# Weighted phase of a mixture-of-experts kernel: the first product by 20 block products for 24, in ten double steps an item

## The chip, the cores and the metric

The kernel runs on one core of a Trainium2 chip. A core has TensorE (PE, matrix products into PSUM), VectorE (DVE), ScalarE (ACT), GpSimd (POOL) and SyncE (SP, which issues most of the DMA transfers). The metric is the device time of one launch in microseconds, the median of three runs.

## The reference

Linear attention with a polynomial sketch makes the tokens x (4352 x 128); then a routing matrix P is normalised over 8 rounds, and 8 experts are applied densely to every token and weighted by P. The second half matters here:

```python
logits = x @ w_gate
P = np.exp(logits - logits.max())
for _ in range(8):
    P /= P.sum(1, keepdims=True) + 1e-09
    P /= P.sum(0, keepdims=True) + 1e-09
    P *= N / E
for e in range(E):                       # 8 experts, D = 128, F = 1024
    h = np.maximum(x @ w1[e], 0.0)       # first product
    ye = h @ w2[e]                       # second product
    out += P[:, e:e + 1] * ye
```

All is float32. As P is positive, P[:, e] can be multiplied into x before the first product.

## The kernel before

Three stages follow each other. Until about 183 us of the profile, attention and routing are computed, with the experts that need no weight before the first product mixed in as filling (`fill`, `steps`). The rest is the **weighted phase** (`weighted`, line 1088 on), which the change rewrites.

**Items.** The weighted phase handles a list `witems` of 60 pairs (group of tokens g, expert e). A group has 2n tokens: groups 0 to 4 have n = 256 and 7 experts each (items 0 to 34), groups 5 to 8 have n = 224 and 6 experts (items 35 to 58), and a last one has n = 224 and a single expert (item 59). Neighbouring groups run through the experts in opposite directions, so an expert's weights serve two items at a border.

**The first product of an item** is x (2n tokens, 128 inputs) by w1 (128 inputs, 1024 columns). Inputs are cut into two halves of 64 rows, tokens into two blocks of n, and columns into blocks; a fast scheme of the 2 x 2 x 2 kind computes 7 products of sums for 8. `firsts(t)` does one half of the columns (s = 0 or 1) of an item, so each item has two such turns of 7 *steps*. A step is four matmuls of 64 x 64 weights, in the four quarters of the PE array, with n moving columns each (in float32 each is issued as two instructions, so a step shows as x8). The steps alternate between two PSUM pairs (`pairs`); after each step ACT or DVE takes the pair out: ACT copies (lines 1204, 1208, 1211) and ReLUs (1135), and DVE's TENSOR_ADD_SAT (line 1138, shown as CUSTOM_DVE_ANT_0), which adds a PSUM operand and a copy and applies the ReLU. A pair can be written again only when it was taken out.

**The second product** (`seconds`, matmuls of line 1271) is also 7 steps for each half; `seconds(t - 1)` alternates step by step with `firsts(t)`. It needs four differences of h, made by DVE (lines 1181 to 1186), whose operands both lie in SBUF.

**Operands of the first product.** `weigh(i + 2, ...)` multiplies the tokens by the row of P on POOL (line 1048), and two DMAs swap the halves of the partitions (line 1051); `sum_x` makes four sums of x, one double sum on POOL (line 1056) and two on DVE (lines 1058, 1060). x has three buffers (`xf`). Before such a POOL operation stands a `gate`: ACT copies one element of the step's output over an element that the POOL operation writes (line 1148), so POOL's operation can't start before that step.

Sums of w1 (*forms*) are made once for each expert, in the seven items of group 0 (`fresh`): `load_raw` (line 936, four DMAs) brings the raw blocks, `sum_first` (lines 960 to 964) makes the sums on POOL, and `store_first` stores seven forms to DRAM. Later items load them back (`load_first`, line 940), in pieces as soon as a step has read the room. There are two buffers of forms (`w1x`), used in turn.

**Order.** In the weighted phase the order of every engine's queue is the order of the code. Each queue is in order: a waiting instruction holds up those behind it. SP's DMAs stand in the same program order. Just before the phase, operands of items 0 and 1 are made ready (the lines from `open_forms()` on), where a planner orders SP and POOL. When a group ends, `finish_seven` and `out_of` make some ten sums of finished results as `leisure`; POOL (in `aside`, once an item half and twice in the last groups) and DVE (in `spare`) take them one by one; `chores` multiply earlier results by their weights on POOL.

Of the kernel before, what the change touches and what calls it, by code (L numbers as in the profile page):

```python
# [52 lines left out]
def kernel(  # L53
# [849 lines left out]
    late = []  # L903
    forms, form_stores, weights, sources = {}, {}, {}, {}
    FORM = FO * H2 // 2

    PLACE = {f: n for n, f in enumerate((0, 4, 5, 7, 6, 2, 3, 1))}
# [3 lines left out]
    def open_forms():  # L911
        w1 = [late[0].tile([P, 8, FORM], F32, name=f"w1x{k}", bufs=1) for k in range(2)]
# [17 lines left out]
    def load_raw(i):  # L930
        w, e = forms[i], witems[i][1]
        for r in range(2):
            for k in range(2):
                rows = H2 * (r ^ k)
                a, b = PLACE[2 * k], PLACE[2 * k + 1]
                nc.sync.dma_start(out=w[0][H2 * r:H2 * (r + 1), a:b + 1:b - a],
                                  in_=moe_w1[e][rows:rows + H2].rearrange("p (i r n) -> p r i n", i=2, r=2)[:, r])
# [18 lines left out]
    def sum_first(i, parts=(0, 1)):  # L956
        g = nc.gpsimd
        w1 = {f: forms[i][0][:, n] for f, n in PLACE.items()}
        if 0 in parts:
            g.tensor_tensor(w1[4], w1[1], w1[3], op=Alu.add)  # L960
            g.tensor_tensor(w1[6], w1[0], w1[1], op=Alu.subtract)
        if 1 in parts:
            g.tensor_tensor(w1[5], w1[4], w1[0], op=Alu.subtract)
            g.tensor_tensor(w1[7], w1[2], w1[5], op=Alu.subtract)

    def store_first(i):
        nc.sync.dma_start(out=form_stores[witems[i][1]][0], in_=forms[i][0][:, 0:7])

    def second_forms():
# [9 lines left out]
        for e in range(1, E):  # L979
            form_stores[e] = (dram.tile([P, 7, FORM], F32, name=f"w1x{e}"),  # L980
# [61 lines left out]
    def weigh(i, gate):  # L1042

        lo, n, _ = wgroups[witems[i][0]]
        xf = sources[i] = late[0].tile([P, 8 * NW], F32, tag="xf", name="xf", bufs=3)[:, 0:8 * n].rearrange(
            "p (b n) -> p b n", b=8)
        gate(xf[:, 0, 0:1])
        nc.gpsimd.tensor_tensor(xf[:, 0:2].rearrange("p b n -> p (b n)"), xT[:, lo:lo + 2 * n], weights.pop(i),  # L1048
                                op=Alu.mult)
        for s in range(2):  # L1050
            in_turn(i, nc.sync.dma_start(out=xf[H2 * (1 - s):H2 * (2 - s), 2:4], in_=xf[H2 * s:H2 * (s + 1), 0:2]))

    def sum_x(i, part_):
        xf = sources[i]
        if part_ == 0:
            nc.gpsimd.tensor_tensor(xf[:, 4:6], xf[:, 1:4:2], xf[:, 0:2], op=Alu.subtract)  # L1056
        elif part_ == 1:
            nc.vector.tensor_tensor(xf[:, 6], xf[:, 3], xf[:, 4], op=Alu.subtract)
        else:
            nc.vector.tensor_tensor(xf[:, 7], xf[:, 2], xf[:, 6], op=Alu.subtract)  # L1060
# [27 lines left out]
    def weighted():  # L1088
# [4 lines left out]
        copies = late[0].tile([P, 2, 3, 2 * NW], F32, name="copies", bufs=1)  # L1093
        leisure, chores = [(lambda engine, do=do: do(), False) for do in left], []
        acc, counts, ending = {}, {}, []
        todo = [(i, s) for i in range(len(witems)) for s in range(2)]

        def flat(t, n):
            return t.rearrange("p (r n) -> p r n", r=2)

        def rooms(t):
            n = wgroups[witems[todo[t][0]][0]][1]
            base = hb[:, 4096 * (t % 2):4096 * (t % 2 + 1)]
            return [base[:, 2048 * a:2048 * a + 8 * n].rearrange("p (b n) -> p b n", b=4) for a in range(2)]

        def firsts(t):

            i, s = todo[t]
            g, e = witems[i]
            n = wgroups[g][1]  # L1110
            a, c = pairs[::-1] if t % 2 and i else pairs
            w1, xf = forms[i][0], sources[i]
            h, ts = rooms(t)
            pa, pc = a[:, :, 0:n], c[:, :, 0:n]
            p1, p5, u2 = (copies[:, t % 2, m, 0:2 * n] for m in range(3))

            def product(out, form, x, start, stop):
                for r in range(2):
                    rows = slice(H2 * r, H2 * (r + 1))
                    for col in range(2):  # L1120
                        o = P * s + H2 * col
                        nc.tensor.matmul(out[H2 * col:H2 * (col + 1), r], w1[rows, PLACE[form], o:o + H2], xf[rows, x],  # L1122
                                         start=start, stop=stop, tile_position=(H2 * r, H2 * col), skip_group_check=True)

            coming = next_of(i, 2) if s else None

            def fetch(lo, hi):
                if coming is not None and coming not in fresh:
                    load_first(coming, lo, hi)

            def add(out, x, y):
                nc.vector.tensor_tensor(flat(out, n), x, flat(y, n), op=Alu.add)

            def relu(x, y):
# [476 lines left out]
```

## Time and profile before

| | before |
|---|---|
| median of 3 runs | 885.81 us (885.80 to 885.93) |
| profiled execution | 886.26 us, of which the profile's span is 884.4 |
| granted TensorE clock, mean | 1.00 |
| DMA, mean over the span | 202 GB/s |
| weighted phase, first to last step of PE | about 188.9 to 879 us |

How to read it: the page comes from one execution. PE, PEld (weight loads, which overlap PE), DVE, ACT and POOL are engines; "x" is a count of instructions; an arrow `out<-in` names the tiles. In a list by time a row has its start, its length (or that of a merged run), engine, line, operation and tiles, and in brackets the idle time before it and what ended it. Successive DVE or POOL operations can overlap by some hundredths of a microsecond, so start-to-start is the better cost of one in a run. The chain that ended last is followed back from the last instruction to whatever released each step.

### The profile page before, as it was taken

To read this page: it belongs to the slowest core of one execution; us is meant where nothing else is said; L and a number is where in the kernel's file an instruction comes from. 1 tells how busy PE (TensorE), PEld (TensorE's weight loads), DVE (VectorE), ACT (ScalarE), POOL (GpSimd) and SP (SyncE) were. 2 spreads that over 40 slices of the span, in tenths; PEclk is the share of its full clock that TensorE was granted. 3 is DMA by queue.
4 is the path that set the end of the run, shared out by engine and by line. 5 is a ranking of instruction groups with operands and counts; after the bars stand their busy time and mean duration, and the time that the engine had idled before them with its cause. 6 is when DMAs were issued, how large, how long until landed. Compare 5 with 4: busy or idle time off the path is not lost.

```text
span 884.4 us, 36157 instructions
## 1 busy us (share of the span) xinstructions
PE 879.0 (99%) x15308; PEld 655.6 (74%) x15308; DVE 762.0 (86%) x1344; ACT 402.9 (46%) x854; POOL 270.0 (31%) x317
## 2 busy tenths in 40 slices
PE   9999999999999999999999999999999999999998
PEld 6788656878887777677767777767877887877786
DVE  8699689977888988888888888888899899899986
ACT  3455457644444344444344344344444444444443
POOL 3131116444451232322222322331332232242411
PEclk9999999999999999999999999999999999999999
DMA  8889299887886776476667777665775975875871
GB/s 256 273 282 272 76 226 249 131 243 209 239 265 201 238 206 200 138 216 204 182 154 204 205 183 198 194 181 161 231 227 150 256 223 146 233 237 138 238 206 31
DMA packets 146465, 179.08 MB, mean 202 GB/s; under 512 B 55680, under 2 KB 93440, under 8 KB 145920
## 3 DMA queue, kind: packets, MB, share of 16 engines
q1 hardware_dynamic: 138192, 166.30, 65.6%
q0 software_dynamic: 6720, 10.19, 5.7%
q8 instruction: 121, 1.98, 1.0%
q10 hardware_dynamic: 1392, 0.28, 0.2%
q14 instruction: 40, 0.33, 0.1%
HBM read 134.22 MB, written 25.99 MB: 181 GB/s over the span
## 4 chain that ended last, share of the span: by engine, by line
PE 98%; DMA 1%; SPq 0%; DVE 0%; issue 0%
PE pair L1122 39%; PE s L1271 39%; PE a L772 9%; PE s L836 7%; PE a L336 1%; PE a L465 1%; DMA qx<-in_q_dram 0%; DMA v<-in_v_dram 0%; PE a L429 0%; PE a L306 0%; PE s L395 0%; PE s L1287 0%; PE s L375 0%; PE a L499 0%; SPq L173 0%; PE a L375 0%
## 5 line engine op out<-in xcount | busy, mean ns | idle before, releaser
L1122 PE MATMUL pair<-xf,w1x 64*64 64x256 f32 (+1 forms) x6736 | 498.6, 366 | 0.0
L1122 PEld LDWEIGHTS pair<-xf,w1x 64*64 64x64 f32 x6736 | 258.5, 133 | 88.9 <-DVE hb L1138 3.8
L1138 DVE CUSTOM_DVE_ANT_0 hb<-pair,copies 128x512 f32<-128x512 f32 (+1 forms) x354 | 234.5, 663 | 73.8 <-ACT xf L1148 30.9
L1271 PE MATMUL s<-hb,w 64*64 64x256 f32 (+1 forms) x3824 | 284.6, 365 | 0.0
L1271 PE MATMUL s<-hb,ws 64*64 64x256 f32 (+1 forms) x2848 | 212.3, 365 | 0.0
L1135 ACT ACTIVATE hb<-pair 128x512 f32<-128x512 f32 (+1 forms) x126 | 72.5, 576 | 287.7 <-PE pair L1122 287.3
L1271 PEld LDWEIGHTS s<-hb,w 64*64 64x64 f32 x3824 | 149.7, 133 | 46.5
L1048 POOL TENSOR_TENSOR xf<-xT,pb 128x512 f32<-128x512 f32 (+1 forms) x60 | 73.4, 1223 | 243.8 <-ACT xf L1148 208.7
L1056 POOL TENSOR_TENSOR xf<-xf 128x512 f32<-128x512 f32 (+1 forms) x59 | 72.0, 1220 | 221.8 <-ACT xf L1148 166.9
L1271 PEld LDWEIGHTS s<-hb,ws 64*64 64x64 f32 x2848 | 111.8, 133 | 34.4
L772 PE MATMUL a<-xT,w 128*64 128x416 f32 (+3 forms) x512 | 122.9, 466 | 0.0
L774 ACT ACTIVATE hb<-a 128x416 f32<-128x416 f32 (+3 forms) x128 | 59.5, 468 | 65.8 <-PE a L772 59.3
L1181 DVE TENSOR_TENSOR hb<-hb 128x512 f32<-128x512 f32 (+1 forms) x118 | 80.4, 682 | 7.0 <-ACT hb L1135 3.0
L1211 ACT COPY copies<-pair 128x512 f32<-128x512 f32 (+1 forms) x118 | 66.5, 563 | 30.3 <-PE pair L1122 30.3
L1208 ACT COPY copies<-pair 128x512 f32<-128x512 f32 (+1 forms) x118 | 66.5, 563 | 29.9 <-PE pair L1122 29.9
L1184 DVE TENSOR_TENSOR hb<-hb 128x512 f32<-128x512 f32 (+1 forms) x118 | 77.3, 655 | 3.0
L1186 DVE TENSOR_TENSOR hb<-hb 128x512 f32<-128x512 f32 (+1 forms) x118 | 79.8, 676 | 0.0
L1185 DVE TENSOR_TENSOR hb<-hb 128x512 f32<-128x512 f32 (+1 forms) x118 | 78.7, 667 | 0.0
L1204 ACT COPY copies<-pair 128x512 f32<-128x512 f32 (+1 forms) x118 | 66.6, 564 | 26.4 <-PE pair L1122 26.4
L836 PE MATMUL s<-hb,ws 128*64 128x416 f32 (+3 forms) x224 | 71.6, 475 | 0.0
L787 DVE TENSOR_TENSOR hb<-hb 128x416 f32<-128x416 f32 (+7 forms) x84 | 56.8, 679 | 14.6 <-ACT hb L774 11.8
L772 PEld LDWEIGHTS a<-xT,w 128*64 128x64 f32 x512 | 54.5, 137 | 19.0 <-issue 7.2
(193 smaller groups left out, 637.1 us busy)
## 6 DMA issues: line engine op xcount, KB each, us to landing
w1x<-w1x SPq DMA_DIRECT2D x135, 256.0 KB, 3.9
w<-w2x SPq DMA_DIRECT2D x103, 256.0 KB, 3.8
ws<-w2x SPq DMA_DIRECT2D x51, 256.0 KB, 4.0
pb<-pT SPq DMA_DIRECT2D x35, 256.0 KB, 4.2
xf<-xf SPq DMA_DIRECT2D x70, 128.0 KB, 3.1
ws<-w2x SPq DMA_DIRECT2D x52, 128.0 KB, 4.0
w1x<-w1x SPq DMA_DIRECT2D x7, 896.0 KB, 6.3
w1x<-w1x SPq DMA_DIRECT2D x45, 128.0 KB, 3.8
```

What stands on the lines that cost most here:

```text
L772: nc.tensor.matmul(ph[sl], loaded_w[j][0][:, P * f + H2 * s:P * f + H2 * (s + 1)], xT[:, at + lo:at + hi], start=True, stop=True, tile_pos ...
L836: nc.tensor.matmul(sums[g][i][H2 * s:H2 * (s + 1)], w, x, start=c == 1, stop=c == per, tile_position=(0, H2 * s))
L1048: nc.gpsimd.tensor_tensor(xf[:, 0:2].rearrange("p b n -> p (b n)"), xT[:, lo:lo + 2 * n], weights.pop(i), op=Alu.mult)
L1056: nc.gpsimd.tensor_tensor(xf[:, 4:6], xf[:, 1:4:2], xf[:, 0:2], op=Alu.subtract)
L1122: nc.tensor.matmul(out[H2 * col:H2 * (col + 1), r], w1[rows, PLACE[form], o:o + H2], xf[rows, x], start=start, stop=stop, tile_position=(H ...
L1135: nc.scalar.activation(out=x, in_=y, func=Act.Relu)
L1138: nc.vector._custom_dve(TENSOR_ADD_SAT, out=flat(out, n), in0=x, in1=flat(y, n), s0=math.inf, s1=0.0)
L1181: nc.vector.tensor_tensor(ts[:, 0], h[:, 3], h[:, 0], op=Alu.subtract)
L1184: nc.vector.tensor_tensor(ts[:, 2], h[:, 1], ts[:, 0], op=Alu.subtract)
L1185: nc.vector.tensor_tensor(ts[:, 1], h[:, 3], h[:, 1], op=Alu.subtract)
L1186: nc.vector.tensor_tensor(ts[:, 3], h[:, 2], ts[:, 2], op=Alu.subtract)
L1271: yield lambda rho=rho, rows=rows, c=c: nc.tensor.matmul(acc[g][rho][q][H2 * half:H2 * (half + 1), n * place:n * (place + 1)], w[rows], fl ...
```

## The change

The first product of an item is no longer split into two halves of columns with 7 products each. It is cut into 3 blocks of tokens, 2 halves of inputs and 4 blocks of 256 columns, and computed by 20 block products instead of 24. A token block has m = ceil(2n / 3) tokens: 171 for n = 256, 150 for n = 224, with the few missing ones filled by zeros. Forms of w1 are now 20 blocks of 128 columns a partition; the x buffer holds 20 blocks of m.

- **PE**: `firsts(i)` has ten *double steps*, each of two block products (8 matmuls of m columns) that lie side by side in one PSUM pair. Between them stand one or two steps of the second product, now both halves of the item before: (1, 2, 1, 1, 1, 2, 2, 2, 1, 1).
- **ACT and DVE** take each double step out with the lists in the code below. ACT also copies a sum back into a PSUM pair once an item (`nc.scalar.copy(both, z_u)`).
- **x**: eight sums instead of four (`sums_of_x`), six of them on POOL at the head of the item before, two on DVE in double steps 6 and 8. There are two x buffers for three, and `weigh(i + 1)` runs at the head of item i (for `weigh(i + 2)` in its middle). The one-element copies (`gate`) are gone.
- **w1**: `load_raw` issues eight DMAs for four; `sums_of_w` makes the forms with seven POOL and three DVE operations in the items of group 0, and for items 0 and 1 with twelve POOL operations each ahead of the phase. 20 blocks are stored and loaded for 14 (7 forms of 2).
- **item 0** uses the eight raw blocks, which are loaded a second time into the `copies` tile for it, in 16 steps of n columns as before, but without steps of a second product between them.
- Differences of h get their room from six slots; adding up a finished group's second half is put off to double step 1 of the next item; finished results are summed in the tiles of the earlier phase, on POOL twice and on DVE once an item.

The core of the diff, shortened:

```diff
+    STEPS = (((0, 1), (1, 4)), ((2, 5), (3, 3)), ((4, 17), (5, 15)), ((6, 0), (7, 7)), ((8, 9), (9, 10)),
+             ((10, 16), (11, 12)), ((12, 19), (13, 18)), ((14, 14), (15, 13)), ((16, 6), (17, 2)), ((18, 8), (19, 11)))
...
+        x_slots.extend(late[0].tile([P, 20 * BLOCK], F32, name=f"xf{k}", bufs=1) for k in range(2))
...
+    def sums_of_w(i, alone=False):
...
+        return [add((6, 9), (18, 19), (12, 1), Alu.subtract),
+                lambda: g.tensor_tensor(pick(w, 4, 8), pick(w, 0, 18), pick(w, 6, 0), op=Alu.subtract),
+                minus,
+                one(11, 7, 15, Alu.subtract),
+                add((5, 10), (1, 14), (7, 6)),
+                add((2, 3), (15, 14), (10, 11), Alu.subtract),
+                one(16, 1, 4, Alu.subtract),
+                one(17, 5, 0),
+                negate]
...
+        return [sum_(x[:, 0], x[:, 1], x[:, 3], Alu.subtract),
+                sum_(x[:, 8:10], x[:, 2:4], x[:, 5:7]),
+                sum_(x[:, 10:12], x[:, 5:7], x[:, 2:4], Alu.subtract),
+                sum_(x[:, 7], x[:, 4], x[:, 5]),
+                sum_(x[:, 16:18], pick(x, 5, 9), x[:, 0:2], Alu.subtract),
+                sum_(x[:, 14:16], pick(x, 2, 4), pick(x, 0, 10)),
+                sum_(x[:, 12:14], pick(x, 3, 6), x[:, 7:8].to_broadcast([P, 2, m]), Alu.subtract),
+                sum_(x[:, 18:20], pick(x, 15, 17), pick(x, 1, 4), Alu.subtract)]
...
+            if new:
+                if i:
+                    weigh(i + 1)
+                xs = sums_of_x(i + 1)
+                xs[0](nc.gpsimd)
+                for do in ws[0:2]:
+                    do()
+                for do in xs[1:6]:
+                    do(nc.gpsimd)
...
+            both, one, other = products(1, True)
+            if i in fresh:
+                store_first(i)
+            nc.scalar.mul(ns15, other, -1.0)
+            add_relu(h(0, 1), one, ns15)
+            while put_off:
+                put_off.pop(0)()
+            before(0, 2, 1, 3)
+            yield
+            both, one, other = products(2, True)
+            fetch(2)
+            nc.scalar.copy(s13_17, both)
+            before(1, 0, 2)
+            yield
+            both, one, other = products(3, False)
+            nc.scalar.copy(z_u, both)
+            yield
+            both, one, other = products(4, True)
+            fetch(4)
+            nc.scalar.mul(s19_16, both, -1.0)
+            before(1, 1)
+            aside(False)
+            yield
+            both, one, other = products(5, False)
+            add_relu(h(2, 3), one, s19_16[:, :, 0])
+            add_relu(h(1, 2), other, s19_16[:, :, 1])
+            for do in ws[2:8]:
+                do()
+            yield
+            both, one, other = products(6, False)
+            fetch(6)
+            add(t2_t, both, s13_17)
+            add(t2_t[:, :, 1], t2_t[:, :, 1], t2_t[:, :, 0], Alu.subtract)
+            before(1, 3)
+            if new:
+                xs[6](nc.vector)
+            yield
+            both, one, other = products(7, False)
+            relu(h(0, 3), one)
+            relu(h(0, 2), other, -1.0)
+            nc.scalar.copy(both, z_u)
+            aside(True)
+            yield
+            both, one, other = products(8, False)
+            fetch(8)
+            add_relu(view(hb, 24 * BLOCK * (i % 2) + m, (3 * m, 2), (1, 2 * m)), pairs[0][:, :, 0:2 * m],
+                     c[:, 0:4 * m].rearrange("p (r n) -> p r n", r=2))
+            if new:
+                xs[7](nc.vector)
+            for do in ws[8:9]:
+                do()
+            if g and new:
+                for _ in range(2 if g in (1, LAST - 1) else 1):
                     leave(nc.vector, True)
             yield
+            both, one, other = products(9, False)
+            add_relu(h(2, 1), one, s19_16[:, :, 0])
+            add_relu(h(1, 1), other, s19_16[:, :, 1])
+            relu(h(0, 0), t2_t[:, :, 1])
             if ending:
                 add_half(ending[0], 0)
...
+            both, one, other = products(10, False)
+            fetch(10)
+            relu(h(1, 3, (2, 2)), both, -1.0)
+            sum_of_h(i, 0, (0,))
             yield
...
+            for many, _ in zip((1, 2, 1, 1, 1, 2, 2, 2, 1, 1), f):
+                for _ in range(many):
+                    next(s, None)
...
-        weigh(0, lambda x: None)
+        weigh(0)
+        load_raw(0, copies[0][:, 0:8 * FB].rearrange("p (k n) -> p k n", n=FB))
         for part_ in range(4):
             load_second(0, part_)
-        weigh(1, lambda x: None)
+        weigh(1)
         load_weights(2)
         load_raw(1)
-        sum_first(1)
-        sum_x(1, 0)
-        sum_first(0)
+        for do in sums_of_w(1, True):
+            do()
+        for do in sums_of_w(0, True):
+            do()
         store_first(0)
```

More of the change, by code (lines that the diff above doesn't have):

```diff
@@ L1109, in firsts @@
+        def firsts(i):
             g, e = witems[i]
-            n = wgroups[g][1]
-            a, c = pairs[::-1] if t % 2 and i else pairs
+            n, m = wgroups[g][1], block_of(i)
             w1, xf = forms[i][0], sources[i]
[L1113 to L1123, printed above, removed]
```

396 lines of the change are left out of this document (208 added, 188 removed).

## The prediction

> **What bounds the kernel now.** I read the page's shares and the chain that ended last, then PE's steps in order of time, then the queues of VectorE (DVE) and GpSimd (POOL) beside them.
>
> ```profile
> span 884.4 us, 36157 instructions
> ...
> PE 879.0 (99%) x15308; PEld 655.6 (74%) x15308; DVE 762.0 (86%) x1344; ACT 402.9 (46%) x854; POOL 270.0 (31%) x317
> ...
> PE 98%; DMA 1%; SPq 0%; DVE 0%; issue 0%
> ```
>
> The chain is PE from end to end; only a shorter PE or a new wait of PE can move the time. One weighted item, of 28 PE steps, in a view by stretches (the stretch and its length; busy time and instructions of PE, PE's weight loads, DVE, ACT and POOL; then TensorE's granted clock):
>
> ```profile
> 308.81:320.90 12.09, 12.09 (x232) 8.56 (x228) 10.04 (x18) 5.10 (x10) 3.94 (x4) 1.00 0.70 200
> ```
>
> PE never pauses, at full clock, but DVE works 10.0 of 12.1 us: it has 2 us to spare. PE's steps, first of an item with blocks of 256 tokens, then of 224:
>
> ```profile
> 399.30 0.61 PE L1271 MATMUL s<-hb,w 64*64 64x256 f32 x8
> ...
> 401.89 0.61 PE L1271 MATMUL s<-hb,w 64*64 64x256 f32 x8
> ...
> 642.58 0.56 PE L1271 MATMUL s<-hb,ws 64*64 64x224 f32 x8
> ...
> 644.85 0.37 PE L1271 MATMUL s<-hb,w 64*64 64x224 f32 x4
> ```
>
> Six steps lie between the first and the last of each pair: 0.432 us a step at 256 columns, 0.378 at 224. The line through both is 1.67 ns a column plus 5 ns a step: columns set PE's time.
>
> **What PE gains.** The new blocks have 171 (of 512 tokens) or 150 (of 448) columns: 0.290 and 0.255 us a step. Twenty for fourteen: 5.80 for 6.04 (0.24 less) in the 34 items of 256 after item 0, 5.10 for 5.30 (0.20 less) in the 25 of 224. Item 0 keeps its 16 steps. Sum: 34 x 0.24 + 25 x 0.20 = **13.2 us less**. An item then asks 11.84 or 10.40 us of PE.
>
> Per item PE issues 48 more matmul instructions (two passes each). The shortest matmuls of the trace bound what one costs beside its columns:
>
> ```profile
> 30.17 2.10 PE a L336 x72
> ```
>
> These have 64 columns (27 ns by the slope: 64 x 1.67, over four) and take 29 each, so 2 ns at most, 0.1 us an item, 6 us in all; at least it is the 5 ns a step already counted. I take the latter, which was measured in this tiling.
>
> The Trainium skill, "TensorEngine Tiling (Array Packing)", section Performance Considerations, gives each matmul about 60 cycles of overhead, which speaks against cutting products smaller. By it 48 more instructions would cost, as an estimate at the 2.4 GHz of the Trainium skill's "TensorE: Matmul & The Clock Gate" (its opening table), 1.2 us an item, 71 us in all, and turn the gain into a loss. The trace's 29 ns for a whole matmul of 64 columns does not bear it out where matmuls are queued.
>
> **What DVE and POOL get instead.** Their costs, first alone:
>
> ```profile
> 399.15 0.41 DVE L1381 TENSOR_TENSOR y<-z,w 64x256 f32<-64x256 f32 x1
> 399.49 0.68 DVE L1184 TENSOR_TENSOR hb<-hb 128x512 f32<-128x512 f32 x1
> 400.09 0.68 DVE L1185 TENSOR_TENSOR hb<-hb 128x512 f32<-128x512 f32 x1
> ...
> 226.82 1.46 DVE L1138 CUSTOM_DVE_ANT_0 hb<-pair,copies 128x512 f32<-128x512 f32 x2 [0.52 <-ACT xf L1148]
> ...
> 226.78 1.28 POOL L1048 TENSOR_TENSOR xf<-xT,pb 128x512 f32<-128x512 f32 x1 [4.23 <-ACT xf L1148]
> 228.02 1.28 POOL L1056 TENSOR_TENSOR xf<-xf 128x512 f32<-128x512 f32 x1
> ```
>
> From start to start DVE takes 0.60 us for 512 elements out of SBUF and 0.34 for 256, so 0.43 for 342 (2 x 171); with one operand in PSUM 0.74 for 512 (1.46 for two, from which half is 0.73), so 0.57 for 342 and 0.92 for 684. New item: eight differences of h (0.60), u and two sums of x (0.43), five add-ReLUs and, of 684, an add and an add-ReLU out of PSUM: 4.8 + 1.3 + 2.85 + 1.85 = 10.8 us, 6.1 of it with both operands in SBUF. The same list before: eight of 512, two of 256, six add-ReLUs, 9.9.
>
> POOL takes 1.24 for 512. That is 0.04 less than the row's 1.28; its undisturbed op of 256, 0.73 in the next fence (232.90), so takes 0.70, and 342 take 0.88, 171 take 0.52. New item: the weighing 1.24, and six sums of x, 4 x 0.88 + 2 x 0.52: 5.8 us, for 2.5 before. ACT has five passes of 684 and four of 342, 4800 elements for 4096, and is half idle above: nothing. Stored forms grow from 14 to 20 blocks of 64 KB an item (the fetches are queued as the steps read their room and have an item's time to land); at the 200 GB/s and 0.70 share of the item above, 2.4 MB, 0.39 MB more make 0.81: nothing.
>
> **The row that decides.** Before, a one-element ACT copy (line 1148) holds POOL's sums back until DVE is in its PSUM work. Where that failed, in the first items, one sees why it is there:
>
> ```profile
> 229.97 0.69 DVE L1184 TENSOR_TENSOR hb<-hb 128x512 f32<-128x512 f32 x1
> 230.57 1.22 DVE L1185 TENSOR_TENSOR hb<-hb 128x512 f32<-128x512 f32 x1
> 231.72 1.21 DVE L1186 TENSOR_TENSOR hb<-hb 128x512 f32<-128x512 f32 x1
> ...
> 230.21 1.04 POOL L960 TENSOR_TENSOR w1x<-w1x 128x256 f32<-128x256 f32 x1 [0.91 <-DMA w1x<-in_moe_w_dram]
> 231.21 1.18 POOL L961 TENSOR_TENSOR w1x<-w1x 128x256 f32<-128x256 f32 x1
> 232.90 0.73 POOL L963 TENSOR_TENSOR w1x<-w1x 128x256 f32<-128x256 f32 x1 [0.52 <-ACT w1x L1148]
> ```
>
> Beside the two add-ReLUs of 226.82, above, POOL's op keeps its 1.28 and they their 0.73. Beside a DVE op out of SBUF alone, both are long: 1.22 for 0.69, 1.18 for 0.73. They take turns, whole instruction by whole instruction, each waiting 0.5 us for the other. The change removes every such copy. DVE's 6.1 and POOL's 5.8 exclude each other: 11.9 us of turns in an item of 11.84, before POOL's one or two sums of finished results an item (0.70 each) and DVE's one (0.34).
>
> Place of the collisions: POOL weighs as soon as the last double step of the item before has read its slot; the two swaps land about 1.1 + 3.1 us after that (rows below); so its sums of x run back to back from about 4 to 8.5 us into the item. There DVE has two differences of h, then (after PSUM work) u, a difference and a sum of x: five ops, each waiting between nothing and 0.67 us (0.53 scaled from 256 to 342). I take half, 1.7; all of it is 3.4. DVE also stands about 0.8 at the head of an item: its first add-ReLU needs the double step (0.58) and ACT's negation (0.5, from the row below) and has one difference (0.6) to do meanwhile.
>
> ```profile
> L1204 ACT COPY copies<-pair 128x512 f32<-128x512 f32 x43 | 25.3, 588 | 10.7 <-PE pair L1122 10.7
> ```
>
> Item: 10.8 + 0.8 + 1.7 = 13.3 us against PE's 11.84. Queued behind a waiting DVE op are the add-ReLUs that free the two PSUM pairs, so PE waits at double steps 7, 8, 10 and the next 1. At 224 tokens DVE's list is 9.7, with 0.75 and 1.5 it is 11.9 against 10.40. Over 28 items and 24: 28 x 1.45 + 24 x 1.5 = **77 us more**. Bounds: nothing (POOL falls under PSUM work throughout), and 14.4 and 12.5 with the sums of finished results and longer waits, 122 us.
>
> **The first seven items** also load raw weights and sum them while the phase runs: eight transfers for four, on SP's queue ahead of the swaps.
>
> ```profile
> L936 SPq DMA_DIRECT2D w1x<-in_moe_w_dram x28: 533/584/1792, 178.2 to 251.2; - x28
> w1x<-in_moe_w_dram SPq DMA_DIRECT2D x28, 128.0 KB, 3.9
> xf<-xf SPq DMA_DIRECT2D x70, 128.0 KB, 3.1
> ```
>
> The first row is one line's issues (shortest, median, longest ns), the next two the transfers' size and median time to landing; from the queue in order of time:
>
> ```profile
> 227.75 0.58 SPq L1040 DMA_DIRECT2D pb<-pT  x1
> ...
> 228.90 1.15 SPq L1051 DMA_DIRECT2D xf<-xf  x2
> ```
>
> From the last read of the buffer: eight issues at 0.584, the last lands at 4.1 + 3.9 = 8.0; two sums of w (1.4) to 9.4; five sums of x (4.0) to 13.4, the swaps having landed by 8.9; three sums of 0.43, 0.70, 0.70 and the one DVE's negation needs (0.43), to 15.7; negation 0.34 and two add-ReLUs queued behind it 1.14: 17.2, where PE would start the next item at 12.3 (a step of 0.43 and an item). As buffers alternate, this chain spans two items, 2.5 us each at least; POOL's queue, which is one, carries the lateness on, 5 each. I take 5 for five items: **25 us** (bounds 12 and 30).
>
> **The start.**
>
> ```profile
> 184.14 1.01 SPq L950 DMA_DIRECT2D w<-w2x  x2
> 185.24 0.85 SPq L953 DMA_DIRECT2D ws<-w2x  x2
> ...
> 188.89 4.33 PE L1122 MATMUL pair<-xf,w1x 64*64 64x256 f32 x72
> ```
>
> SP begins the raw loads at 178.2. Now: 4.7 for item 0, swaps 1.2, 4.7 again into copies, landed at 192.1; PE's first product moves from 188.9 to there. Second forms 1.9, swaps 1.1, weights 0.6, item 1's eight: the last lands at 200.4; twelve POOL sums (7 x 0.70, 5 x 0.43) end at 207.5, and PE, done with item 0 at 199.0 (16 x 0.432), waits for them. 3.2 + 8.5: **12 us** (bounds: 0, if SP and POOL get these done beside the phase before; 16, with sums of x behind them).
>
> **Sum.** The profiled execution took 886.3 (span 884.4, 1.9 around it; median of runs 0.45 lower): 886.3 - 13.2 + 12 + 25 + 77 = 987.
>
> **Rivals.** (1) Faster: POOL's sums fall beside PSUM work and the loads are early; PE stays the bound: 886.3 - 13.2 = 873. For it: DVE's list fits 11.84 with 1 us over, and nothing before stalls PE. Against: half of DVE's list collides. It decides where DVE waits under 11.84 - 10.8 - 0.8 = 0.2 us an item. (2) Only start and first items cost, later items are PE's: 886.3 - 13.2 + 12 + 15 (five items of 3, no turns) = 900. For it: those items alone have POOL's sums of w. (3) Turns at their upper bound: 886.3 - 13.2 + 12 + 30 + 122 = 1037. For it: results of the group before are summed in nearly every item. (4) A matmul's fixed cost is what shows, 6 us on PE: gain 7, 879 without the rest; a chance of 0.03.
>
> **Chances.** Forecast 0.50, (1) 0.10, (2) 0.20, (3) 0.17, (4) 0.03. The likeliest's own range is 950 to 1020; with (2) and (3) the range is 895 to 1037. Differences under 0.2% (1.8 us) cannot be told from none: faster 0.13, within 0.02, slower 0.85.
>
> **What would show it.** Right: DVE ops out of SBUF of 342 and 512 elements with means far above 0.5 and 0.69 us; POOL's 342-wide above 0.9; PE idle before double steps with DVE as releaser in every item; items about 13 us apart; PE starting its weighted work near 192 and idle before item 1. Wrong: PE at 99% with steps of 0.29 us, or PE waiting for a DMA or ACT. A step well above 0.29 would break the gain itself.

## The result, and the profile after

The changed kernel takes 1100.71 us (median of 4 runs, 1098.11 to 1105.50) against 885.80: a ratio of 1.243, with a 95% interval of 1.239 to 1.248. The forecast was 987 and its range ended at 1037. The direction was right, and the loss is twice the one forecast. From the page of the changed kernel (1101.99 us in this execution): its span, the engines' busy time, TensorE's granted clock in 40 slices, the chain of waits by engine, two groups of instructions (busy time, mean ns, idle time before them and what ended it), and the swaps (KB, median us to landing).

```profile
span 1100.2 us, 42014 instructions
...
PE 940.9 (86%) x18140; PEld 779.0 (71%) x18140; DVE 915.4 (83%) x1461; ACT 419.6 (38%) x783; POOL 543.1 (49%) x663
...
PEclk9999999889899999999989999998899999889899
...
PE 38%; POOL 18%; DVE 17%; DMA 14%; issue 7%; SPq 5%; ACT 1%; POOLq 0%; DVEq 0%; ACTq 0%
...
L1104 POOL TENSOR_TENSOR xf<-xf 128x171 f32<-128x171 f32 (+1 forms) x354 | 300.7, 876 | 339.1 <-DMA xf<-xf 302.9
...
L1104 DVE TENSOR_TENSOR xf<-xf 128x342 f32<-128x342 f32 (+1 forms) x118 | 113.7, 964 | 52.2 <-POOL xf L1104 44.2
...
xf<-xf SPq DMA_DIRECT2D x70, 128.0 KB, 4.2
```

The chain was PE from end to end before. Now 54% of it is POOL, DVE, DMA and SP's queue. POOL, busy only half the time, stands 303 us waiting for the swaps, and DVE then waits 44 us for POOL. The turns that the prediction looked for are there too; by shape, in the same form:

```profile
L1104 POOL TENSOR_TENSOR xf<-xf 128x342 f32<-128x342 f32 x136 | 136.8, 1026 | 178.0 <-DMA xf<-xf 161.1 <-PE pair L1199 11.5 <-PE s L1368 5.3
...
L1104 DVE TENSOR_TENSOR xf<-xf 128x342 f32<-128x342 f32 x68 | 66.1, 972 | 26.7 <-POOL xf L1104 18.9 <-DMA w1x<-in_moe_w_dram 7.8
L1213 DVE CUSTOM_DVE_ANT_1 hb<-pair,copies 128x342 f32<-128x342 f32 x136 | 66.0, 506 | 7.8 <-PE pair L1199 6.4
L1176 DVE TENSOR_TENSOR hb<-hb 128x512 f32<-128x512 f32 x71 | 57.0, 802 | 0.4
```

DVE's 342-wide sum of x takes 0.97 us where the add-ReLU of the same width out of PSUM takes 0.51, and a difference of h takes 0.80 for 0.68 before.

**Where the time went.** Item starts are the first matmul of double step 1. Item 7 starts at 315.8; with PE alone it would be 188.9 + 16 x 0.432 + 6 x 11.84 = 266.8, so 49 us are lost by then. Items 7 to 34 are 15.11 us apart on average (PE asks 11.84) and items 35 to 58 14.05 (10.40): 28 x 3.27 + 24 x 3.65 = 179 us. With the 13.2 that PE gains, 886.3 + 49 + 179 - 13.2 = 1101. So nearly all of the miss lies in the steady items, forecast at 13.3 and 11.9.

One of them, in time: PE's double steps 1, 10 and the next 1, then DVE, POOL and SP (start, length, in brackets the idle time before and what ended it).

```profile
526.85 0.81 PE L1199 MATMUL pair<-xf,w1x 64*64 64x171 f32 x16 [0.94 <-DVE hb L1213]
...
539.32 0.81 PE L1199 MATMUL pair<-xf,w1x 64*64 64x171 f32 x16 [1.39 <-DVE hb L1213]
541.65 0.81 PE L1199 MATMUL pair<-xf,w1x 64*64 64x171 f32 x16 [1.08 <-DVE hb L1213]
```
```profile
537.34 1.14 DVE L1104 TENSOR_TENSOR xf<-xf 128x342 f32<-128x342 f32 x1 [2.06 <-POOL xf L1104]
538.40 0.86 DVE L1213 CUSTOM_DVE_ANT_0 hb<-pair,copies 128x684 f32<-128x684 f32 x1
539.18 1.01 DVE L1104 TENSOR_TENSOR xf<-xf 128x342 f32<-128x342 f32 x1
540.12 0.43 DVE L1526 STREAM_TRANSPOSE yt<-m 128x256 f32<-128x256 f32 x1
540.48 1.02 DVE L1213 CUSTOM_DVE_ANT_1 hb<-pair,copies 128x342 f32<-128x342 f32 x2
```
```profile
524.99 1.54 POOL L1095 TENSOR_TENSOR xf<-xT,pb 128x512 f32<-128x512 f32 x1
...
535.05 4.09 POOL L1104 TENSOR_TENSOR xf<-xf 128x342 f32<-128x342 f32 x5 [7.40 <-DMA xf<-xf]
539.10 0.72 POOL L1484 TENSOR_TENSOR m<-m,kept 128x256 f32<-128x256 f32 x1
539.79 1.00 POOL L1131 TENSOR_TENSOR kept<-kept,pk 128x256 f32<-128x256 f32 x1
540.75 1.27 POOL L1095 TENSOR_TENSOR xf<-xT,pb 128x512 f32<-128x512 f32 x1
```
```profile
528.07 0.42 SPq L1078 DMA_DIRECT2D pb<-pT  x1
528.53 1.38 SPq L1127 DMA_DIRECT2D pk<-pT  x1
530.01 1.11 SPq L1097 DMA_DIRECT2D xf<-xf  x2
```

Read it as a round. The weighing ends at 526.53. Its swap stands on SP behind stores and loads and is issued 3.5 later; two issues take 1.1; it lands after 3.9; POOL's five sums take 4.1, results and a chore 1.6, and the next weighing starts 15.8 after the last. DVE closes it to PE: its two sums of x need POOL's, and queued behind the second are the add-ReLUs (540.48) that free the pair for the next step 1. Over the items 8 to 32 the means are 1.36 (weighing), 1.44 (SP), 1.11, 4.25 (landing), 4.73 (sums), 2.23 to the next weighing: 15.1, the length of an item. These pieces follow one queue from one weighing to the next, so they add up to an item whatever limits it; that they do is no proof, and the experiments have to show what holds the round. In 15 of the weighings POOL waits, 33 us in all, for PE's last step on the buffer. PE's own loss (items 10 to 33, start to start, against 0.58 a double step and 0.432 a step of the second product) is 1.6 us an item before step 1, 0.7 before step 10 and 0.3 before step 7, all of them steps that wait for DVE.

### The profile page after: what moved, and what is told of

It reads as the page before. It is cut to its first block, busy times and chain, and to the rows that moved or that the text cites. A ratio compares the mean times of both kernels' runs of the same rounds, so it can differ in the third digit from the quotient of the medians.

```text
span 1100.2 us, 42014 instructions
## 1 busy us (share of the span) xinstructions
PE 940.9 (86%) x18140; PEld 779.0 (71%) x18140; DVE 915.4 (83%) x1461; ACT 419.6 (38%) x783; POOL 543.1 (49%) x663
## 4 chain that ended last, share of the span: by engine, by line
PE 38%; POOL 18%; DVE 17%; DMA 14%; issue 7%; SPq 5%; ACT 1%; POOLq 0%; DVEq 0%; ACTq 0%
PE pair L1199 14%; PE s L1368 11%; DMA xf<-xf 11%; POOL xf L1104 10%; PE a L772 6%; PE s L836 4%; DVE w L1176 4%; DVE hb L1213 4%; POOL xf L1095 3%; DVE xf L1104 3%; DVE hb L1176 2%; SPq L944 1%; SPq L1097 1%; DMA w<-w2x 1%; DVE copies L1207 1%
## 5 line engine op out<-in xcount | busy, mean ns | idle before, releaser
L1199 PE MATMUL pair<-xf,w1x 64*64 64x171 f32 (+1 forms) x9440 | 479.6, 314 | 147.4 <-DVE hb L1213 70.0
L1199 PEld LDWEIGHTS pair<-xf,w1x 64*64 64x64 f32 x9440 | 376.0, 140 | 234.6 <-DVE hb L1213 76.9
L1104 POOL TENSOR_TENSOR xf<-xf 128x171 f32<-128x171 f32 (+1 forms) x354 | 300.7, 876 | 339.1 <-DMA xf<-xf 302.9
L1368 PE MATMUL s<-w,ws 64*64 64x256 f32 (+1 forms) x1888 | 190.3, 365 | 0.5 <-issue 0.5
L1104 DVE TENSOR_TENSOR xf<-xf 128x342 f32<-128x342 f32 (+1 forms) x118 | 113.7, 964 | 52.2 <-POOL xf L1104 44.2
L1176 DVE TENSOR_TENSOR w<-hb 128x512 f32<-128x512 f32 (+1 forms) x197 | 146.9, 762 | 2.0 <-PE s L1368 1.9
L1213 DVE CUSTOM_DVE_ANT_0 hb<-pair,copies 128x342 f32<-128x342 f32 (+1 forms) x118 | 77.8, 659 | 63.3 <-ACT copies L1274 62.2
L1213 DVE CUSTOM_DVE_ANT_1 hb<-pair,copies 128x342 f32<-128x342 f32 (+1 forms) x236 | 107.8, 486 | 12.2 <-PE pair L1199 10.0
L1368 PEld LDWEIGHTS s<-w,ws 64*64 64x64 f32 x1888 | 96.4, 133 | 3.9 <-issue 0.9
L1368 PE MATMUL s<-w,w 64*64 64x256 f32 (+1 forms) x624 | 94.7, 376 | 0.0
L1176 DVE TENSOR_TENSOR hb<-hb 128x512 f32<-128x512 f32 (+1 forms) x119 | 89.4, 752 | 1.1 <-PE s L1368 0.4
```

Of the source, the lines that this page charges most:

```text
L1104: return lambda engine: engine.tensor_tensor(out, a, b, op=op)
L1176: nc.vector.tensor_tensor(own[a], x, y, op=Alu.subtract)
L1199: nc.tensor.matmul(pair[H2 * col:H2 * (col + 1), r, m * j:m * (j + 1)], w1[rows, form, H2 * col:H2 * (col + 1)], xf[rows, x], start=start ...
L1213: nc.vector._custom_dve(TENSOR_ADD_SAT, out=out, in0=x, in1=y, s0=math.inf, s1=0.0)
L1368: yield lambda rho=rho, rows=rows, c=c: nc.tensor.matmul(acc[g][rho][q][H2 * half:H2 * (half + 1), n * place:n * (place + 1)], w[rows], x[ ...
```

## The experiments

The theories: **turns** (what the prediction priced: DVE and POOL keep each other out of SBUF), **chain** (the round above) and **clock** (PE's clock falls to half after idle time). Two numbers behind each time are the mean distances of the items 7 to 34 and 35 to 58 (changed kernel: 1100.7 us; 15.11 and 14.05). The changed kernel's own runs differ by 7 us, so differences below that are not read as gain or loss.

**e1: POOL's five sums write without reading.**

```diff
-                for do in xs[1:6]:
-                    do(nc.gpsimd)
+                for out_, a_, b_ in holds(i + 1):
+                    nc.gpsimd.tensor_tensor(out_[..., 0:1], a_[..., 0:1], b_[..., 0:1], op=Alu.add)
+                    for _ in range(2):
+                        nc.gpsimd.memset(out_, 0.01)
```

> The five sums of x that POOL makes after the swap become, each, a sum of one column (it waits for the same data) and two fills of the same output, which read nothing from SBUF; their results are constants. Turns (POOL and DVE exclude each other): DVE's four or five waits of 0.5 to 0.8 us an item are gone, items of 15.1 and 14.05 us fall to about 12.5 and 11.8, the kernel to 960 to 1000. Chain (weighing one item ahead is too late): POOL's stretch is as long as before, so 1070 to 1100.

1106.5 us (14.86, 14.59). Rows of its groups by shape:

```profile
L1182 DVE TENSOR_TENSOR hb<-hb 128x512 f32<-128x512 f32 x71 | 51.2, 721 | 1.1 <-PE s L1376 0.7
...
L1104 DVE TENSOR_TENSOR xf<-xf 128x342 f32<-128x342 f32 x68 | 47.7, 701 | 51.7 <-POOL xf L1252 42.1 <-DMA w1x<-in_moe_w_dram 9.2
```

DVE's operations are short again (0.72 for 0.80, 0.70 for 0.97), as the Trainium skill, "SBUF — State Buffer", section SBUF: two separate sides, has it: a DVE operation with two SBUF inputs is locked out only by a GpSimd operation that reads SBUF. But what DVE no longer loses in turns it waits for POOL's end (42 us for 19 in this shape), and the time stays. With the round closed, taking these turns away alone brings nothing. The edit is not quite even: the writes take 5.30 us an item where the sums took 4.73 (means of items 10 to 34), and that lengthens the round.

**e2: no swaps from item 7 on.**

```diff
-        for s in range(2):
+        for s in range(2 if i < 7 else 0):
```

> From item 7 on the two swap transfers of x are left out (the sums read old data). POOL's sums then follow the weighing at once, some 5.7 us earlier (303 us of POOL's waits for these transfers over 53 items). Chain: items fall to about 13.3 and 11.9, what DVE's list asks with its waits, the kernel to 970 to 1010. Turns: as many collisions at other places, 1060 to 1110.

1087.9 us (15.24, 13.37), though the swap, 6.8 us of the round with its wait on SP, is gone. POOL's sums now follow the weighing at once, into double steps 1 to 5, where DVE makes its differences of h:

```profile
PE 43%; DVE 36%; issue 7%; POOL 5%; DMA 3%; SPq 3%; ACT 2%; ACTq 0%; POOLq 0%; DVEq 0%
...
L1199 PE MATMUL pair<-xf,w1x 64*64 64x171 f32 (+1 forms) x9440 | 461.5, 308 | 141.4 <-DVE hb L1213 107.0
```
```profile
L1176 DVE TENSOR_TENSOR hb<-hb 128x512 f32<-128x512 f32 x71 | 69.8, 983 | 0.8 <-PE s L1368 0.4
```

A difference takes 0.98 for 0.80, DVE has 36% of the chain for 17%, and PE waits for its add-ReLUs, now before step 7. So the swap's delay had kept POOL off DVE's busiest stretch.

**e8: both at once, no swaps and no reading.**

> Leaves out the swap DMAs from item 7 on, and GpSimd's five sums after them are writes without reading, of about the same length. This takes both suspects away at once: no wait for the swap, no collision of the five sums with VectorE. If the two together are the whole price of the steady items, these come to 11.8 to 12.4 and 10.4 to 11 us, and the time to 925 to 965 us (item 7 still starts near 316 us). If something else carries it (the clock, or VectorE's own list), 1020 to 1090 us.

961.6 us (12.54, 11.43). Alone the two edits bring -6 and 13 us, together 139: each hides the other's price.

**e3: matmuls on constants ahead of each step 1, to keep PE warm.**

```diff
+            for _ in range(8):
+                for r in range(2):
+                    rows = slice(H2 * r, H2 * (r + 1))
+                    for col in range(2):
+                        nc.tensor.matmul(pairs[1][H2 * col:H2 * (col + 1), r, 352:480], ones[rows, 0:H2],
+                                         ones[rows, 0:P], start=True, stop=True, tile_position=(H2 * r, H2 * col),
+                                         skip_group_check=True)
             both, one, other = products(1, True)
```

> Eight extra steps of 128 columns (1.75 us, on constants, into unused columns of a PSUM pair) stand before each item's first double step, where PE idles 1.7 us on average. Clock: if the half-speed clock after idle time costs what PE's busy time suggests (941 us where columns ask 866), the granted clock goes to 0.99 and the kernel to 1020 to 1060. If the clock only runs beside other waits: 1090 to 1130.

1172.6 us (16.41, 15.23), clock 0.981 for 0.947. It settles nothing: the added matmuls waited for the add-ReLUs that step 1 waits for,

```profile
L1275 PE MATMUL pair<-ones 64*64 64x128 f32 x3776 | 128.3, 289 | 66.0 <-DVE hb L1213 64.7
```

and so came on top. The price of the half clock by itself stays open; an estimate is below.

**e4: finished results (their sums, weights and stores) left out**, in `aside`, in step 8 and at the end.

> The sums, weights and stores of finished results (POOL twice and DVE once an item) are left out. Turns: 0.7 us of POOL's port twice and 0.34 of DVE an item are gone; by the difference of the prediction's two cases (14.4 and 13.3, 12.5 and 11.9) 45 us less, and up to 70 with what the clock adds: 1030 to 1055. Chain: POOL's results stand behind its sums and before the next weighing, 1070 to 1095.

1018.9 us (13.66, 12.23): more than either theory gave. The round shows why: until the next weighing 0.81 us for 2.23, SP's wait 1.23 for 1.44, and DVE has one operation less in front of the add-ReLUs.

**e13: DVE's two sums of x at the end of the item.** DVE's two sums of x are needed in steps 6 and 7 of the *next* item only. Here they are behind the add-ReLUs that free PE's pairs; nothing is left out, and POOL and SP are as they were.

```diff
-            if new:
-                xs[6](nc.vector)      # step 6
...
-            if new:
-                xs[7](nc.vector)      # step 8
...
             relu(h(0, 0), t2_t[:, :, 1])      # step 9
+            if new:
+                xs[6](nc.vector)
...
             sum_of_h(i, 0, (0,))      # step 10
+            if new:
+                xs[7](nc.vector)
```

> One edit of the changed kernel: VectorE's two x sums stay in their item, but stand behind the add-ReLUs of step 9 and behind step 10, where they block only the first add-ReLU of the next item, which that item's step 3 needs. All is still computed; GpSimd and SyncE are as in the changed kernel. Chain theory: the loop gets some 3 us of room (steps 1 and 2), and VectorE's first half of the item isn't made longer as it was by the sums in steps 3 and 4: 1000 to 1040 us, 1046 or better. If the loop still binds through step 3: 1060 to 1090 us. Turns theory alone: 1085 to 1110 us.

1032.6 us (13.96, 12.91): 68 us for the order of two instructions in one queue. These sums (second row) hardly wait for POOL any more:

```profile
L1176 DVE TENSOR_TENSOR hb<-hb 128x512 f32<-128x512 f32 x71 | 57.7, 813 | 1.5 <-PE s L1368 1.0
...
L1104 DVE TENSOR_TENSOR xf<-xf 128x342 f32<-128x342 f32 x68 | 51.3, 755 | 9.5 <-DMA w1x<-in_moe_w_dram 8.9 <-POOL xf L1104 0.7
```

The turns are still there (a difference of h takes 0.81): turns alone can't have been the 68. But the edit does two things. From item 7 to the last, DVE waited 39 us for POOL's sums and 48 us for ACT's negation at the head of an item, where it had little else to do; in e13 both waits are gone, since a sum of x now fills the second (28 us of waits for POOL's results come in their place). e5, below, takes away the wait for POOL, leaves 29 us of that for ACT, and gains 54. PE's time at half clock falls too, from 119 to 51 us, which at half speed is up to 34 of the 68; it follows the waits.

**e6 and e14: POOL's results under the swap's wait**, on the changed kernel (e6) and on e13 (e14).

```diff
                 xs[0](nc.gpsimd)
+                if i:
+                    aside(False)
+                    aside(True)
```

with the two calls in steps 4 and 7 gone.

> The two finished-result sums that GpSimd makes in each item are put between the weighing and the five x sums, into the time in which GpSimd waits for the swap, in place of behind the five sums and ahead of the next weighing. All is still computed. Chain theory: about 2 us of GpSimd work leave the loop, of which the part on the path comes back, 1040 to 1080 us. Turns theory: 1085 to 1110 us, since the number of collisions is the same.

> The x sums at the end of the item, and the results of GpSimd under the swap's wait. Chain theory: the loop is open with 4 to 5 us of room, 985 to 1025 us, below the kernel with the sums in steps 3 and 4 (1029). If the results collide with VectorE's differences there for as much as they free, as much as the run before (within 10 us).

e6 1086.5 us (14.64, 13.85), between the two theories; e14 1010.5 (13.24, 12.74). So 14 and 22 us. Stretches 400 to 600 of the changed kernel, then of e14 (busy us and instructions of PE, PE's weight loads, DVE, ACT and POOL; granted clock; DMA's share and GB/s):

```profile
400.00:600.00 200.00, 173.87 (x3648) 146.11 (x3640) 177.08 (x258) 75.35 (x126) 107.25 (x115) 0.95 0.62 175
```
```profile
400.00:600.00 200.00, 193.30 (x4207) 160.58 (x4201) 193.87 (x296) 87.57 (x147) 121.95 (x132) 1.00 0.71 200
```

PE and DVE are now both at 97%: what is left is mostly DVE's load, collisions included (e18, below), and the clock is full again by itself in this stretch. POOL's way from one weighing over the swap and the sums to the next has little room either: it idles only 0.50 us an item ahead of the weighing (items 10 to 34).

**e5 and e7: a poorer place for DVE's two sums, steps 3 and 4 of the next item**, without (e5) and with (e7) the results moved.

> The two x sums that VectorE makes (form pairs 12/13 and 18/19) are needed only by double steps 6 and 7 of the next item; here VectorE makes them in the next item's steps 3 and 4, so that the add-ReLUs of step 9, which free the PSUM pair for the next item's step 1, no longer stand behind them. All is still computed. Chain theory (weighing, swap, GpSimd sums, VectorE's sums, add-ReLUs, next step 1 make a closed loop of some 15 us per item): the loop is opened, the items fall to what VectorE's list asks, 12.5 to 13.5 and 11 to 12 us, and the time to 990 to 1040 us. Turns theory (VectorE and GpSimd stretch each other at SBUF, and that alone is the price): the same operations collide somewhere else, 1085 to 1110 us. Clock theory (the half clock after idle time sets the size): 1070 to 1100 us.

> Both edits together, x sums of VectorE in the next item and results under the swap's wait. Chain theory: 980 to 1030 us, no more than 15 us better than the x sums moved alone, since the loop is open by then. Turns theory: 1080 to 1110 us.

1046.4 (14.17, 13.00) and 1028.7 us (13.80, 12.71). They open the round too, but lengthen DVE's list ahead of the add-ReLUs of step 5, so that PE waits before step 7. Four edits of e7:

**e9 (no reading), e10 (weighing and swap right behind step 9), e11 (no sums of raw weights for items 2 to 6), e12 (POOL's sums held by a one-element ACT copy behind step 4, as before the change).**

```diff
+            if i + 2 < len(witems):      # e10, in step 9
+                weigh(i + 2)
...
-            ws = sums_of_w(i + 1) if 1 < i + 1 in fresh else []      # e11
+            ws = []
...
+            if new and i + 1 not in fresh:      # e12, in step 4
+                nc.scalar.copy(sources[i + 1][:, 8, 0:1], s19_16[:, 0, 0, 0:1])
+                for do in xs[1:6]:
+                    do(nc.gpsimd)
```

> The kernel with both edits (VectorE's x sums in the next item, results under the swap's wait), and in it GpSimd's five sums are writes without reading of about the same length; the swaps stay. Turns theory, once the loop is open: VectorE no longer waits for GpSimd's five sums, the items come from 13.8 and 12.7 us to about 12.4 and 11.3, and the time from 1029 to 955 to 985 us, near the 962 of the kernel without swaps and reading. If the swaps and SyncE's queue still hold the items: 1005 to 1030 us.

> The kernel with both edits, and the weighing of the next item is put in the order right behind double step 9 of this one, so that its swap stands on SyncE's queue ahead of the fetches of step 10, the second forms and the next weights. If the loop through the swap is open already, this changes nothing: 1018 to 1034 us. If it still binds, about 1.2 us per item come back: 965 to 1000 us.

> The kernel with both edits, without the sums of raw weights for items 2 to 6 made during the phase (items 1's stay, ahead of it). Prediction's step: five items give back 5 us each, items 2 to 6 come 25 us earlier, 1000 to 1008 us. If VectorE's and GpSimd's turns over the x sums hold those items as they hold the later ones: 6 to 12 us less, 1016 to 1023 us.

> The kernel with both edits, and from item 7 on GpSimd's five sums wait for a one-element copy of ScalarE behind double step 4, as the kernel before held them back; they then run from about 5.5 to 10 us into the item, where VectorE mostly reads PSUM. All is still computed. Turns theory: the waits of VectorE's differences of h for GpSimd go, part of the collisions stays (one difference, u), 985 to 1015 us. If the place of the collisions doesn't matter: 1022 to 1040 us.

e9 1011.1 us (13.21, 12.59): 18 us, where the turns theory gave 44 or more. But its writes take 5.28 us for the 4.55 of e7's sums, and POOL then weighs at once (0.02 us idle on average), so 18 is not the price of the turns. e11 1023.2: item 7 starts at 300.2 for 310.5, so the form sums cost these five items 10 us, not 25. Without them items 3 to 6 are still 15 us apart, where the later ones of e11 are at 13.83: their raw loads are still there, the swaps wait 2.7 to 7.2 us on SP, and POOL goes from its sums straight to the next weighing. e12 1025.0 (13.57, 12.61): no gain to be told. e10 missed both theories: 1113.4 us (15.82, 13.34). The swap lands in a median 2.4 us, and POOL's sums come 2 us earlier, onto the differences of h; POOL, then DVE of e10:

```profile
595.56 5.67 POOL L1104 TENSOR_TENSOR xf<-xf 128x342 f32<-128x342 f32 x5 [0.69 <-DMA xf<-xf]
```
```profile
595.95 1.28 DVE L1177 TENSOR_TENSOR hb<-hb,w 128x512 f32<-128x512 f32 x1
597.15 1.40 DVE L1177 TENSOR_TENSOR w<-hb 128x512 f32<-128x512 f32 x1
```

It is e2 once more: 5.7 us for sums of 4.1, 1.3 and 1.4 for differences of 0.7. A shorter chain, 85 us slower than e7.

**e15 to e18, all with DVE's sums at the end of the item:** e15 is e14 without reading in POOL's five sums, e16 e14 with the ACT copy, e17 e13 without results, e18 e14 without the differences of h:

```diff
-                nc.vector.tensor_tensor(own[a], x, y, op=Alu.subtract)
+                own[a] = h[a]
```

> As the run before, and GpSimd's five sums are writes without reading of about the same length; the swaps stay. Turns theory with the loop open: 20 to 50 us less than the run before, at 950 to 990 us. If no loop and no turns of these five sums are left, within 10 us of it.

> The x sums of VectorE at the end of the item, results under the swap's wait, and from item 7 on GpSimd's five sums wait for a one-element copy of ScalarE behind double step 4, as the kernel before held them. All is still computed. Turns theory: fewer waits of VectorE in its differences of h, 5 to 25 us less than the kernel without the copy. If the later sums close the loop again, 10 to 40 us more.

> VectorE's x sums at the end of the item, and the sums, weights and stores of the finished groups' results left out. Chain theory: with the loop closed, leaving the results out brought 82 us; with the loop open it brings only what they collide and cost VectorE, 20 to 50 us below the 1010 of the kernel with results under the swap's wait: 960 to 990 us. If what is left there is VectorE's own list: 990 to 1008 us.

> VectorE's x sums at the end of the item, results under the swap's wait, and the eight differences of h left out (TensorE takes plain blocks of h in their place, as many steps): 4.8 of VectorE's 10.8 us per item go, and nearly all that the weighing and the results collide with. If VectorE's list with its waits is what holds the items at 13.2 and 12.7 us, they come to 12 to 12.4 and 10.6 to 11 us, 940 to 970 us. If the swap's way (weighing, swap, sums) still holds them: 985 to 1010 us.

e15 1006.4 us (13.07, 12.67) and e16 1011.2 (13.25, 12.78): no gain beyond the spread, where 20 to 50 were expected of e15. That does not make the turns cheap. DVE is busy 184.27 us of the stretch 400 to 600 in e15, for 193.87 in e14, and the time hardly moves, because now POOL's own way is as long as an item:

```profile
525.95 0.20 POOL L1253 TENSOR_TENSOR xf<-xf 128x2 f32<-128x2 f32 x1 [5.82 <-DMA xf<-xf]
...
530.40 0.82 POOL L1255 MEMSET xf<- 128x342 f32 x2
531.18 1.59 POOL L1095 TENSOR_TENSOR xf<-xT,pb 128x512 f32<-128x512 f32 x1
...
543.57 1.28 POOL L1095 TENSOR_TENSOR xf<-xT,pb 128x512 f32<-128x512 f32 x1
```

The writes take 5.39 us for the 4.53 of e14's sums, POOL idles 0.04 us before the next weighing, and from item 7 on DVE waits 20 us for POOL's end (5 in e14). What the turns of the five sums cost by themselves stays open.

e17 960.0 (12.50, 11.49) is 73 us below e13 and 50 below e14; e18 963.5 (12.44, 11.65) is 47 below e14. In e18 DVE is busy only 112.80 us of the stretch 400 to 600, PE 196.71: DVE's list, with what collides with it, did hold e14. How much of e17's gain is collisions, and how much the results' own operations and DMA traffic, the runs don't separate. No version beats the kernel before; e14, the best that computes everything, is 125 us behind.

## Why the prediction was wrong, step by step

- **PE's gain**: right. A double step and the step of the second product behind it start 0.58 us apart where nothing holds PE, two times 0.290; no fixed cost of a matmul shows.

```profile
518.33 0.79 PE L1199 MATMUL pair<-xf,w1x 64*64 64x171 f32 x16
518.91 0.64 PE L1368 MATMUL s<-w,ws 64*64 64x256 f32 x8
```

- **The start**: nearly right. PE's weighted phase starts at 192.59 (192.1 forecast); item 1's first product then waits, as forecast, for POOL's twelve sums, which end at 210.9, not 207.5: the five sums of x ran ahead of them (the upper bound had them behind).

```profile
200.96 0.52 PE L1199 MATMUL pair<-xf,w1x 64*64 64x171 f32 x8 [1.17 <-ACT hb L1210]
210.93 0.95 PE L1199 MATMUL pair<-xf,w1x 64*64 64x171 f32 x8 [9.44 <-POOL w1x L992]
```
```profile
198.99 3.98 POOL L1104 TENSOR_TENSOR xf<-xf 128x342 f32<-128x342 f32 x5 [4.45 <-DMA xf<-xf]
...
210.03 0.84 POOL L992 TENSOR_SCALAR w1x<-w1x 128x256 f32<-128x256 f32 x1
```

- **The first seven items**: start and first items together 49 us, 37 forecast. That the raw loads stand on SP ahead of the swaps was right: the swaps of items 3 to 6 wait 3.6 to 6.6 us there, later ones 1.4. The form sums by themselves are worth 10 us (e11, in the order of e7); what the loads alone cost was not tried.
- **Steady items**: here it failed, in the step "Item: 10.8 + 0.8 + 1.7 = 13.3 us". It adds up DVE's queue as if POOL's sums were there when DVE asks for them. The place of POOL's sums was put "from about 4 to 8.5 us into the item", and nobody was asked to wait for their end. They run from 5.6 to 10.4, because the swap waits on SP (1.4), lands in 4.2 us from its issue and not 3.1 (the rows of the two pages), and the weighing ahead of it stands behind results. Behind their end stand, on DVE's side, its sums of x, the add-ReLUs of step 9 and the next step 1, and in POOL's own queue the results and the next weighing: a round of 15.1 us. With two x buffers, one item of lead and in-order queues this wait is part of the item. Taken away, with POOL's results under the swap's wait (e14), items are at 13.24 and 12.74.
- **The terms of that sum**, from the trace (items 8 to 33, 15.2 us each, every DVE operation counted up to the start of the next): DVE is busy 13.4 us, where list and collisions had 12.5, and idle 1.8 for 0.8. Operations out of SBUF take 8.6, where the list had 6.1 and collisions 1.7; those out of PSUM 3.9 for 4.7; results and sums at a group's end take 0.9, which the sum left out. Of the idle time 1.0 is the wait for ACT's negation (the forecast's 0.8, though its own terms, 0.58 + 0.5 - 0.6, give 0.5) and 0.5 the wait for POOL's sums, which it had at nothing.
- **The cause given for the loss**: the collisions are real, and a little larger than priced, but taking the reading out of POOL's five sums gained nothing while the round was closed (e1); taken away together with the swap's wait it gained 139 us (e8), and the collisions come to the front when POOL is early (e2, e10). Their share alone was not separated. That e14's items stand near 13.3 is in part luck: there too operations out of PSUM are cheaper than reckoned and results come on top.
- **The signs** named as right were seen but for the distance of the items (15.1 and 14.05, not about 13); DVE before the double steps was there too, and they did not tell the two apart. The one that would have was listed as "wrong": a wait for DMA. It was POOL that waited for it, 303 us.
- **Rivals**: the third, 1037, was nearest. It was right to count the results (without them, e4, 82 us less), but the rest it put down to longer waits in turns. None was a round that closes over SP and the swap.

## What to carry to other kernels

When a change shortens a lead (three buffers to two) or lets one engine's output feed back into the same item, follow one item's operand around all queues until it meets itself, and compare that length, without waits for anything outside the round, with the item; busy time says nothing of it. In an in-order queue, put what the next item needs behind what frees a resource now: that was worth 68 us here. Two prices can hide each other: an edit that shows nothing alone (e1, e2) is not free, so take both away before dropping a theory. And an edit that takes a collision away must not lengthen what stands on the path: the writes of e9 and e15 were 0.7 and 0.9 us longer than the sums they stood for, and so hid what they were to show.

## What the runs showed of the hardware

PE's clock fell to half for 119 us in all (e14: 50), mostly in items where PE was at no time idle for as long as such a stretch. Four successive stretches of 3.41 us of the changed kernel, in the columns given for e14:

```profile
491.21:494.63 3.42, 3.42 (x80) 2.60 (x72) 3.39 (x5) 1.54 (x3) 2.64 (x4) 1.00 0.45 111
494.63:498.04 3.41, 1.57 (x33) 0.99 (x33) 3.38 (x6) 1.24 (x2) 1.81 (x2) 1.00 0.82 263
498.04:501.45 3.41, 3.41 (x48) 3.10 (x47) 2.02 (x5) 0.70 (x2) 0.00 (x0) 0.50 0.71 225
501.45:504.87 3.42, 3.42 (x85) 3.15 (x81) 3.11 (x5) 1.96 (x3) 1.70 (x2) 1.00 0.27 81
```

PE worked 1.57 of 3.41 us (46%) in the second, and the third ran at half clock. Between 205 and 930 us, in all 17 such falls of the changed kernel PE's share in the 3.41 us before was 46% or less, and in the 168 stretches that stayed at full clock 45% or more; the clock came back only after stretches of 81% or more. The Trainium skill, "TensorE: Matmul & The Clock Gate", Part 1, says that the clock halves after at least one idle window of about 3.4 us; the length agrees, but here a window less than half busy was enough. An estimate of its price: in the stretch 400 to 600 a matmul takes 173.87 / 3648 = 47.7 ns, in e14 193.30 / 4207 = 45.9; 1.7 ns on 3648 are 6 us of 200, or some 24 in the 760 us of steady items. As the clock is halved, 119 us of it can't have cost more than 60.
